# Hash attention with a gated feed-forward on one core: loads by need on the Pool queue, an eight-tile hash with four bit transfers, one piece of work held back at each block end, and first products placed behind the normalise

## Chip, core, metric

One core of one Trainium2 chip. The metric is the device time of a whole execution in microseconds (us), median of several. The profile's span, from first to last instruction, is 1.7 to 2.1 us shorter than the time of the same execution in the runs shown here.

## The reference, cut to what matters

```python
q_bits = (einsum('bhsd,dk->bhsk', q, proj) > 0); k_bits = ...      # 6 bits per row: a bucket
mask   = q_bucket[..., :, None] == k_bucket[..., None, :]
scores = where(mask, q @ k.T / sqrt(64), -1e9); attn = softmax(scores) @ v
x = attn, heads joined                                             # (3072, 512)
ffn = gelu(x @ w_gate) * (x @ w_val) @ w_out
out = x + sigmoid(x @ w_res) * ffn
```

Four batches, eight heads, 768 positions, head size 64, all fp32 outside the kernel.

## The kernel before

A *pair* is two heads of one batch: 16 pairs. `prep_pair` transposes a pair's q and k on TensorE, hashes them, and builds for each head an augmented matrix: 64 rows of q and k and 7 rows of bits, so that a single product yields score and mask together. The bits are computed across partitions 0 to 127 and must move to partitions 64 to 70: that needs transfers.

A *block* is one batch and half of the queries: 24 attention steps, `scores(i)` then `attend(i-2)`. At a block's end its output is transposed (`transpose_x`) and goes through 12 gate groups; the rest of its feed-forward is cut in pieces and dealt out over the next block's steps. Block 0 has no feed-forward to deal out. The *normalise* divides a pair's finished products by their row sums on VectorE (`rec`, then `xtok`).

The profile names tiles: `sc` are scores, `e` their exponentials on ScalarE, `av` products, `tps` transposes of q and k, `hps` the hash, `aug` the augmented matrix, `xps` the transposes of a block's output, which are copied to `xT`, `gps` gates, and `vps`, `rps`, `ops` the rest of the feed-forward.

```python
load_pair(0)                     # q, k, v on the SP queue
... proj on the ACT queue ...
load_pair(1)

def prep_pair(n):
    ...                          # 12 transposes, copies to trT on ScalarE and VectorE
    hp = mm_psum.tile(...)       # mm_psum has three buffers
    for i in range(4):           # q and k of two heads: four column tiles of 32
        matmul(hp[32*i:32*i+32, 0:CH], proj_pair, trT[:, i*CH:(i+1)*CH])
    tensor_scalar(bits, hp, 0.0, shift, is_gt, subtract)
    for hh, side, par in ...:    # eight transfers
        (scalar if n == 0 and par == 1 else sync).dma_start(a[D:KAUG, ...], bits[row:row+7])
    ...                          # VectorE casts of trT to the 64 upper rows: 4 of 64x768

cast_v(0); drain(prep_pair(0)); cast_v(1); drain(prep_pair(1))
load_pair(2); load_pair(3)       # behind the bit transfers on SP
...
if end_of_block:                 # in the step loop, after attend
    fill(0.8); transpose_x(u); fill(100.0)    # transpose_x: both copies on VectorE
    for m in range(KF): gate(u, m)
    ff = feed_forward(u)         # its last piece ends in y, o on VectorE and a store
```

The softmax here doesn't subtract the row's maximum and nothing guards it: scores larger than these inputs give would overflow.

Of the kernel before, what the change touches and what calls it, by code (L numbers as in the profile page):

```python
# [19 lines left out]
def kernel(  # L20
# [54 lines left out]
    def load_pair(n):  # L75
        b, j = pairs[n]
        for nm, src in (("q", q), ("k", k), ("v", v)):
            s = stage.tile([P, 2, T, D], FP32, tag=nm + "s", name=nm + "s")
            nc.sync.dma_start(
                s, src[b, 2 * j:2 * j + 2].rearrange("h (p t) d -> p h t d", t=T))  # L80
            staged[(nm, n)] = s

    load_pair(0)


# [6 lines left out]
    nc.scalar.dma_start(proj_pair[D:2 * D, NR:NR + NBITS], proj)  # L92
    load_pair(1)

    ind = const.tile([P, 2], FP32, name="ind")
    for side in range(2):
        nc.vector.tensor_reduce(
            ind[:, side:side + 1],
            ident.rearrange("p (h s c) -> p h s c", h=2, s=2)[:, :, side, NBITS:2 * NR:NR],
            axis=AX.XY, op=ALU.add)  # L100
# [7 lines left out]
    NAUG = 2 * H  # L108
    augs = [const.tile([P, 2 * S], BF16, name=f"aug{i}") for i in range(NAUG)]
# [6 lines left out]
    def aug_of(b, h):  # L116
        return augs[(b * H + h) % NAUG]

# [26 lines left out]
    def prep_pair(n):  # L145
# [15 lines left out]
        hp = mm_psum.tile([P, 512], FP32, tag="mm", name="hps")  # L161
        for i in range(4):
            nc.tensor.matmul(hp[32 * i:32 * i + 32, 0:CH], proj_pair, trT[:, i * CH:(i + 1) * CH],  # L163
                             start=True, stop=True)
        bits = s_pool.tile([P, CH], BF16, tag="bits", name="bits")
        nc.vector.tensor_scalar(bits, hp[:, 0:CH], 0.0, shift, op0=ALU.is_gt, op1=ALU.subtract)  # L166
        for hh in range(2):
            a = aug_of(b, 2 * j + hh)
            for side in range(2):
                for par in range(2):  # L170
                    row = 32 * (2 * hh + side) + NR * par
                    eng = nc.scalar if n == 0 and par == 1 else nc.sync
                    eng.dma_start(  # L173
                        a[D:KAUG, side * S + par * CH:side * S + (par + 1) * CH],
                        bits[row:row + NR, :])
        if n == 0:
            cast_aug(n, trT, 0)
            yield
            cast_aug(n, trT, 1)
            return  # L180
        yield
        cast_aug(n, trT, 0)
        yield
        cast_aug(n, trT, 1)
        yield

    def cast_aug(n, trT, hh):
        b, j = pairs[n]
        a = aug_of(b, 2 * j + hh)
        for par in range(2):  # L190
            nc.vector.tensor_scalar_mul(  # L191
                a[0:D, :].rearrange("d (s n) -> d s n", s=2)[:, :, par * CH:(par + 1) * CH],
                trT[par * D:(par + 1) * D, hh * S:(hh + 1) * S].rearrange("d (s n) -> d s n", s=2),
                QKS)
# [5 lines left out]
    LEAD = 2  # L200
    x_tok, xT, gh = {}, {}, {}
    e_tiles, av_tiles = {}, {}

    def scores(i):
        b, c, j, hh, jp = steps[i]
        a = aug_of(b, 2 * j + hh)
        sp = sc_psum.tile([P, 2, 512], FP32, tag="sc", name="sc")
        for x in range(2):
            jt = 2 * jp + x
            nc.tensor.matmul(sp[:, x, 0:CH], a[0:KAUG, S + jt * P:S + (jt + 1) * P],  # L210
                             a[0:KAUG, c * CH:(c + 1) * CH], start=True, stop=True)
        e = e_pool.tile([P, 2, CH], BF16, tag="e", name="e")
        nc.scalar.activation(e, sp[:, :, 0:CH], AF.Exp, scale=EXPS)  # L213
        e_tiles[i] = e
# [30 lines left out]
    def transpose_x(u):  # L245
        xT[u] = x_pool.tile([P, KM, CH], BF16, tag="xT", name="xT", bufs=2)
        for k2 in range(KM // 2):
            ps = mm_psum.tile([P, 1024], BF16, tag="mm", name="xps")
            for x in range(2):
                for t in range(TC):  # L250
# [3 lines left out]
            nc.vector.tensor_copy(xT[u][:, 2 * k2:2 * k2 + 2, :].rearrange("p k n -> p (k n)"),  # L254
                                  ps[:, 0:2 * CH])
# [52 lines left out]
    drain(prep_pair(0))  # L308
    cast_v(1)
    drain(prep_pair(1))  # L310
    load_pair(2)
    load_pair(3)
    run(weights)
    run(weights)


    begin = {2: 1, 3: 7}
    for n in range(4, len(pairs)):
        b, j = pairs[n]
        begin[n] = (b - 1) * 2 * LB + (LB + 6 * j if b == 1 else 12 * j)  # L320
    loads = {}
    for n in range(4, len(pairs)):
        loads.setdefault(max(2, begin.get(n - 3, -6) + 5), []).append(n)

    NS = len(steps)
    RATE = 17.0 / LB
    prep = None
# [3 lines left out]
    ff_next = None  # L331

    def fill(need):

        nonlocal ff
        while need > 0 and ff is not None:
            d = run(ff)
            if d is None:
                ff = None
            else:  # L340
                need -= d
        return need

    for i in range(NS + LEAD):
        if i < NS:
            scores(i)
        if i >= LEAD:
            attend(i - LEAD)

        for n in loads.pop(i, []):  # L350
            load_pair(n)
        if i < 14 * 2 and i % 2 == 0:
            run(weights)
        if prep is None and todo and i >= begin[todo[0]]:
            n = todo.pop(0)
            cast_v(n)
            prep = prep_pair(n)
        if prep is not None:
            if next(prep, "done") == "done":
                prep = None  # L360

        credit += RATE
        if credit > 0:
            credit = fill(credit) if ff is not None else 0.0
        if i >= LEAD and (i - LEAD) % LB == LB - 1:
            u = (i - LEAD) // LB
            fill(0.8)
            transpose_x(u)
            fill(100.0)
# [3 lines left out]
            credit = 0.0  # L373
    drain(ff)
# [30 lines left out]
```

## Time and profile before

| | before |
|---|---|
| time, median of 3 | 413.34 us (412.99 to 416.0) |
| span of the profiled run | 410.1 us |
| TensorE busy | 366.4 us, 89% |
| ScalarE / VectorE / GpSimd busy | 61% / 42% / 6% |
| first scores start | 16.03 us |
| first gate group starts | 64.18 us |

TensorE is the bound, so the thing to look for is where it is not at work, or at work slowly. The *chain of work* is followed back from the last instruction, at each step to what released it. PEclk is the TensorE clock that was granted, as a share of full speed. The ends of matmuls are modelled and overlap the next start.

### The profile page before, as it was taken

The numbers are of one execution on the slowest core, as the hardware profiler recorded it, in microseconds if no ns is written. First come the engines' busy times: TensorE is split into PE (matmuls) and PEld (weight loads), VectorE is DVE, ScalarE is ACT, GpSimd is POOL, SyncE is SP. The second block draws the span as 40 slices with busy tenths as digits, with TensorE's granted clock in tenths as the row PEclk, the third lists the DMA queues.
The fourth block names the chain that finished last, engine by engine and source line by source line (L and its number), as shares of the span: only waits on it lengthen the run. The fifth ranks groups of instructions, "written<-read, shape, count | busy, mean of one in ns | idle before, by whom it ended". The sixth has DMA issues, their size and how long they took to land.

```text
span 410.1 us, 7658 instructions
## 1 busy us (share of the span) xinstructions
PE 366.4 (89%) x3077; PEld 222.5 (54%) x3104; DVE 171.6 (42%) x328; ACT 248.6 (61%) x360; POOL 22.9 (6%) x35
## 2 busy tenths in 40 slices
PE   5348589999989998999989998999999999998995
PEld 3035255655556655565555655565556555654552
DVE  2504302675535654175326453275315331534162
ACT  2226557765657666766857666766767776775510
POOL 1225010001010000000000000000000000000000
PEclk9658859999999999999999999999999999999999
DMA  6669990034611114030500301000100010000001
GB/s 230 121 245 260 247 235 2 3 122 155 225 55 59 62 53 146 1 108 16 170 26 5 119 30 53 0 7 4 56 26 2 11 42 27 2 21 33 27 0 77
DMA packets 21779, 31.59 MB, mean 77 GB/s; under 512 B 2416, under 2 KB 17648, under 8 KB 21744
## 3 DMA queue, kind: packets, MB, share of 16 engines
q1 hardware_dynamic: 18248, 25.84, 18.4%
q0 software_dynamic: 3280, 5.24, 7.1%
q8 instruction: 24, 0.39, 0.4%
q14 instruction: 11, 0.09, 0.1%
q10 hardware_dynamic: 216, 0.02, 0.0%
HBM read 29.36 MB, written 6.29 MB: 87 GB/s over the span
## 4 chain that ended last, share of the span: by engine, by line
PE 80%; DVE 10%; DMA 4%; SPq 2%; issue 2%; ACTq 1%; ACT 0%; DVEq 0%
PE gps L262 16%; PE ops L287 14%; PE sc L210 14%; PE vps L272 13%; PE av L230 8%; PE tps L155 6%; PE rps L280 5%; PE hps L163 4%; DVE aug L191 2%; DMA aug<-bits 2%; DMA ks<-in_k_dram 2%; DVE gh L275 2%; SPq L173 2%; DVE y L292 1%; DVE o L294 1%
## 5 line engine op out<-in xcount | busy, mean ns | idle before, releaser
L213 ACT ACTIVATE e<-sc 128x768 bf16<-128x768 f32 x192 | 153.3, 811 | 73.4 <-PE sc L210 72.9
L210 PE MATMUL sc<-aug 71*128 71x384 bf16 x384 | 98.8, 340 | 6.6 <-DMA aug<-bits 5.5
L275 DVE TENSOR_TENSOR gh<-vps,gh 128x384 bf16<-128x384 f32 x96 | 53.0, 557 | 102.2 <-PE vps L272 89.3
L230 PEld LDWEIGHTS <-e 128*128 128x128 bf16 x1152 | 62.0, 100 | 34.7 <-issue 6.0
L272 PE MATMUL vps<-xT,wv 128*128 128x384 bf16 x384 | 75.2, 326 | 0.0
L262 PE MATMUL gps<-xT,wg 128*128 128x384 bf16 x384 | 64.8, 326 | 10.4 <-DVE xT L254 10.4
L230 PE MATMUL av<-vaug,e 128*128 128x65 bf16 x1152 | 68.5, 197 | 4.2 <-DVE xtok L240 3.9
L287 PE MATMUL ops<-wo,gh 128*128 128x512 bf16 x273 | 68.9, 379 | 0.6 <-issue 0.2
L264 ACT ACTIVATE gh<-gps 128x384 bf16<-128x384 f32 x96 | 47.1, 491 | 36.7 <-PE gps L262 36.7
L210 PEld LDWEIGHTS <-aug 71*128 71x128 bf16 x384 | 37.2, 102 | 37.1 <-DMA aug<-bits 5.6
L262 PEld LDWEIGHTS <-wg 128*128 128x128 bf16 x384 | 37.5, 98 | 36.3 <-issue 13.0
L272 PEld LDWEIGHTS <-wv 128*128 128x128 bf16 x384 | 33.2, 98 | 18.8 <-issue 3.8
L287 PEld LDWEIGHTS <-gh 128*128 128x128 bf16 x288 | 25.3, 98 | 24.1 <-issue 3.1
L191 DVE TENSOR_SCALAR aug<-trT 64x768 bf16<-64x768 f32 x64 | 37.0, 578 | 0.5
L292 DVE SCALAR_TENSOR_TENSOR y<-th,ops 128x512 f32<-128x512 bf16 x24 | 16.5, 688 | 45.8 <-PE ops L287 40.8
L155 PE MATMUL tps<-ident,qs 128*128 128x128 f32 x96 | 21.2, 311 | 12.6 <-DMA qs<-in_q_dram 12.6
L159 ACT COPY trT<-tps 128x512 f32<-128x512 f32 x32 | 18.6, 586 | 21.2 <-issue 9.2
L283 ACT ACTIVATE th<-rps 128x512 bf16<-128x512 f32 x24 | 14.3, 597 | 20.9 <-PE rps L280 20.5
L143 POOL CAST vaug<-vs 128x768 bf16<-128x768 f32 x16 | 14.2, 887 | 206.3 <-DMA vs<-in_v_dram 158.9
L280 PE MATMUL rps<-wr,xT 128*128 128x512 bf16 x84 | 23.4, 379 | 0.5
L166 DVE TENSOR_SCALAR bits<-hps,shift 128x384 bf16<-128x384 f32 x16 | 9.9, 617 | 30.1 <-PE hps L163 29.3
L155 PE MATMUL tps<-ident,ks 128*128 128x128 f32 x96 | 20.8, 306 | 0.5 <-DMA ks<-in_k_dram 0.4
(31 smaller groups left out, 158.6 us busy)
## 6 DMA issues: line engine op xcount, KB each, us to landing
qs<-in_q_dram SPq DMA_DIRECT2D x16, 384.0 KB
ks<-in_k_dram SPq DMA_DIRECT2D x16, 384.0 KB
vs<-in_v_dram SPq DMA_DIRECT2D x16, 384.0 KB
out_dram<-o SPq DMA_DIRECT2D x24, 256.0 KB
aug<-bits SPq DMA_DIRECT2D x124, 5.2 KB
wg<-in_moe_w_gate_dram POOLq DMA_DIRECT2D x4, 384.0 KB, 6.4
wv<-in_moe_w_val_dram POOLq DMA_DIRECT2D x4, 384.0 KB, 11.4
wo<-in_moe_w_out_dram POOLq DMA_DIRECT2D x4, 384.0 KB, 19.8
```

The costliest lines, as they stand in the source:

```text
L155: nc.tensor.transpose(ps[:, i * P:(i + 1) * P], tiles[4 * g + i], ident)
L191: nc.vector.tensor_scalar_mul(a[0:D, :].rearrange("d (s n) -> d s n", s=2)[:, :, par * CH:(par + 1) * CH], trT[par * D:(par + 1) * D, hh * ...
L210: nc.tensor.matmul(sp[:, x, 0:CH], a[0:KAUG, S + jt * P:S + (jt + 1) * P], a[0:KAUG, c * CH:(c + 1) * CH], start=True, stop=True)
L213: nc.scalar.activation(e, sp[:, :, 0:CH], AF.Exp, scale=EXPS)
L230: nc.tensor.matmul(av[:, o:o + D + 1], e[:, x, t * P:(t + 1) * P], va[:, 2 * j + hh, TS[jt], :], start=(first and x == 0 and t == 0), stop ...
L262: nc.tensor.matmul(ps[:, 0:CH], wg[:, kk, m * P:(m + 1) * P], xT[u][:, kk, :], start=(kk == 0), stop=(kk == KM - 1))
L264: nc.scalar.activation(gh[u][:, m, :], ps[:, 0:CH], AF.Gelu)
L272: nc.tensor.matmul(ps[:, 0:CH], wv[:, kk, m * P:(m + 1) * P], xT[u][:, kk, :], start=(kk == 0), stop=(kk == KM - 1))
L275: nc.vector.tensor_mul(sl, ps[:, 0:CH], sl)
L280: nc.tensor.matmul(rps, xT[u][:, kk, t * P:(t + 1) * P], wr[:, kk, :], start=(kk == 0), stop=(kk == KM - 1))
L287: nc.tensor.matmul(ops, gh[u][:, kk, t * P:(t + 1) * P], wo[:, kk, :], start=(kk == 0), stop=(kk == KF - 1))
L292: nc.vector.scalar_tensor_tensor(y, th, 1.0, ops, op0=ALU.add, op1=ALU.mult)
```

## The change

Intent: have pair 2 and later loaded before they are needed, and off the queue that the bits use; halve the bit transfers, by hashing the two 64-row halves on separate row tiles of the array, so that the two halves of a head's bits lie side by side in the same partitions; and leave TensorE something to do while the last transposes are copied.

```diff
-    load_pair(0)                              # q, k, v
-    ... load_pair(1) ...
+    load_pair(0, nc.sync, "qk"); load_pair(1, nc.sync, "qk")
+    load_pair(0, nc.sync, "v");  load_pair(1, nc.sync, "v")
...
+    load_pair(2, nc.gpsimd)                   # before any preparation
...
-        hp = mm_psum.tile([P, 512], FP32, tag="mm", name="hps")
+        hp = [mm_psum.tile([P, 512], FP32, tag="mm", name="hps") for _ in range(2)]
         for i in range(4):
-            matmul(hp[32*i:32*i+32, 0:CH], proj_pair, trT[:, i*CH:(i+1)*CH])
-        tensor_scalar(bits, hp[:, 0:CH], ...)
-        ... eight transfers of 7 rows x 384
+            for par in range(2):
+                matmul(hp[par][32*i:32*i+32, 0:CH], proj_pair[par*D:(par+1)*D, :],
+                       trT[par*D:(par+1)*D, i*CH:(i+1)*CH])
+        for par in range(2):
+            tensor_scalar(bits[:, par, :], hp[par][:, 0:CH], ...)
+        ... four transfers of 7 rows x 768
-        ... four casts of 64x768
+        ... two casts of 64x1536
...
-            nc.vector.tensor_copy(xT ..., ps)
+            copy = nc.vector.tensor_copy if k2 == 0 else nc.scalar.copy
...
-    load_pair(2); load_pair(3)                # after both preparations
+    load_pair(3, nc.gpsimd)                   # between them; later pairs on Pool too
-        begin[n] = (b-1)*2*LB + (LB + 6*j if b == 1 else 12*j)
+        begin[n] = (b-1)*2*LB + (LB + 6 + 6*j if b == 1 else 8 + 12*j)
-        attend(i - LEAD)
+        # the first product of each pair comes one step later, behind the normalise
-            fill(0.8); transpose_x(u); fill(100.0)
+            fill(99.0, NPIECES - 1); transpose_x(u); fill(99.0, NPIECES)
```

The weights keep to the Pool queue, in larger batches. The number of pieces dealt out over a block's steps is capped, so that three are left for its end.

More of the change, by code (lines that the diff above doesn't have):

```diff
@@ L73, with load_pair @@
     staged = {}
-    def load_pair(n):
+    def load_pair(n, eng, which="qkv"):
         b, j = pairs[n]
-        for nm, src in (("q", q), ("k", k), ("v", v)):
+        for nm in which:
+            src = {"q": q, "k": k, "v": v}[nm]
             s = stage.tile([P, 2, T, D], FP32, tag=nm + "s", name=nm + "s")
-            nc.sync.dma_start(
-                s, src[b, 2 * j:2 * j + 2].rearrange("h (p t) d -> p h t d", t=T))
+            eng.dma_start(s, src[b, 2 * j:2 * j + 2].rearrange("h (p t) d -> p h t d", t=T))
             staged[(nm, n)] = s
-    load_pair(0)
+    load_pair(0, nc.sync, "qk")
+    load_pair(1, nc.sync, "qk")
+    load_pair(0, nc.sync, "v")
+    load_pair(1, nc.sync, "v")
     ident = const.tile([P, P], FP32, name="ident")
@@ L91 @@
     nc.scalar.dma_start(proj_pair[0:D, 0:NBITS], proj)
-    nc.scalar.dma_start(proj_pair[D:2 * D, NR:NR + NBITS], proj)
-    load_pair(1)
+    nc.scalar.dma_start(proj_pair[D:2 * D, 0:NBITS], proj)
     ind = const.tile([P, 2], FP32, name="ind")
@@ L98 @@
             ind[:, side:side + 1],
-            ident.rearrange("p (h s c) -> p h s c", h=2, s=2)[:, :, side, NBITS:2 * NR:NR],
+            ident.rearrange("p (h s c) -> p h s c", h=2, s=2)[:, :, side, NBITS:NR],
             axis=AX.XY, op=ALU.add)
@@ L106 @@
     nc.vector.tensor_copy(ident_bf, ident)
-    NAUG = 2 * H
-    augs = [const.tile([P, 2 * S], BF16, name=f"aug{i}") for i in range(NAUG)]
+    load_pair(2, nc.gpsimd)
+    NAUG = 2 * NPAIR
+    augs = [const.tile([P, 2, 2 * S], BF16, name=f"aug{i}") for i in range(NAUG)]
     vaugs = []
@@ L114, with aug_of @@
         vaugs.append(va)
-    def aug_of(b, h):
-        return augs[(b * H + h) % NAUG]
+    def aug_of(b, j):
+        return augs[(b * NPAIR + j) % NAUG]
     wg = const.tile([P, KM, DFF], BF16, name="wg")
@@ L160, in prep_pair @@
             yield
-        hp = mm_psum.tile([P, 512], FP32, tag="mm", name="hps")
+        hp = [mm_psum.tile([P, 512], FP32, tag="mm", name="hps") for _ in range(2)]
         for i in range(4):
-            nc.tensor.matmul(hp[32 * i:32 * i + 32, 0:CH], proj_pair, trT[:, i * CH:(i + 1) * CH],
-                             start=True, stop=True)
-        bits = s_pool.tile([P, CH], BF16, tag="bits", name="bits")
-        nc.vector.tensor_scalar(bits, hp[:, 0:CH], 0.0, shift, op0=ALU.is_gt, op1=ALU.subtract)
@@ L167, in prep_pair @@
-        for hh in range(2):
-            a = aug_of(b, 2 * j + hh)
-            for side in range(2):
-                for par in range(2):
-                    row = 32 * (2 * hh + side) + NR * par
-                    eng = nc.scalar if n == 0 and par == 1 else nc.sync
-                    eng.dma_start(
-                        a[D:KAUG, side * S + par * CH:side * S + (par + 1) * CH],
-                        bits[row:row + NR, :])
-        if n == 0:
-            cast_aug(n, trT, 0)
-            yield
-            cast_aug(n, trT, 1)
-            return
@@ L181, in prep_pair @@
-        yield
-        cast_aug(n, trT, 0)
-        yield
-        cast_aug(n, trT, 1)
-        yield
-    def cast_aug(n, trT, hh):
-        b, j = pairs[n]
-        a = aug_of(b, 2 * j + hh)
+            for par in range(2):
+                nc.tensor.matmul(hp[par][32 * i:32 * i + 32, 0:CH], proj_pair[par * D:(par + 1) * D, :],
+                                 trT[par * D:(par + 1) * D, i * CH:(i + 1) * CH], start=True, stop=True)
+        bits = s_pool.tile([P, 2, CH], BF16, tag="bits", name="bits")
@@ L190, in cast_aug @@
+        for par in range(2):
+            nc.vector.tensor_scalar(bits[:, par, :], hp[par][:, 0:CH], 0.0, shift,
+                                    op0=ALU.is_gt, op1=ALU.subtract)
+        a = aug_of(b, j)
+        for i in range(4):
+            eng = nc.scalar if n == 0 and i % 2 == 1 else nc.sync
+            eng.dma_start(a[D:KAUG, i // 2, (i % 2) * S:(i % 2 + 1) * S], bits[32 * i:32 * i + NR])
         for par in range(2):
             nc.vector.tensor_scalar_mul(
-                a[0:D, :].rearrange("d (s n) -> d s n", s=2)[:, :, par * CH:(par + 1) * CH],
@@ L193, in cast_aug @@
-                trT[par * D:(par + 1) * D, hh * S:(hh + 1) * S].rearrange("d (s n) -> d s n", s=2),
-                QKS)
+                a[0:D].rearrange("d h (s p n) -> d (h s) p n", s=2, p=2)[:, :, par, :],
+                trT[par * D:(par + 1) * D, :].rearrange("d (i n) -> d i n", i=4), QKS)
+            if n > 0 and par == 0:
+                yield
+        yield
     steps = [(b, c, j, hh, jp) for b in range(B) for c in range(2) for j in range(NPAIR)
@@ L200 @@
     LEAD = 2
+    PS = 2 * (T // 2)
     x_tok, xT, gh = {}, {}, {}
@@ L205, in scores @@
         b, c, j, hh, jp = steps[i]
-        a = aug_of(b, 2 * j + hh)
+        a = aug_of(b, j)[0:KAUG, hh, :]
         sp = sc_psum.tile([P, 2, 512], FP32, tag="sc", name="sc")
@@ L209, in scores @@
             jt = 2 * jp + x
-            nc.tensor.matmul(sp[:, x, 0:CH], a[0:KAUG, S + jt * P:S + (jt + 1) * P],
-                             a[0:KAUG, c * CH:(c + 1) * CH], start=True, stop=True)
+            nc.tensor.matmul(sp[:, x, 0:CH], a[:, S + jt * P:S + (jt + 1) * P],
+                             a[:, c * CH:(c + 1) * CH], start=True, stop=True)
         e = e_pool.tile([P, 2, CH], BF16, tag="e", name="e")
@@ L253, in transpose_x @@
                                         x_tok[u][:, t, ko * P:(ko + 1) * P], ident_bf)
-            nc.vector.tensor_copy(xT[u][:, 2 * k2:2 * k2 + 2, :].rearrange("p k n -> p (k n)"),
-                                  ps[:, 0:2 * CH])
+            copy = nc.vector.tensor_copy if k2 == 0 else nc.scalar.copy
+            copy(xT[u][:, 2 * k2:2 * k2 + 2, :].rearrange("p k n -> p (k n)"), ps[:, 0:2 * CH])
     def gate(u, m):
@@ L308 @@
     drain(prep_pair(0))
+    load_pair(3, nc.gpsimd)
     cast_v(1)
-    drain(prep_pair(1))
-    load_pair(2)
-    load_pair(3)
-    run(weights)
-    run(weights)
-    begin = {2: 1, 3: 7}
+    prep = prep_pair(1)
+    for _ in range(4):
+        run(prep)
+    for _ in range(KM):
+        run(weights)
+    begin = {2: 0, 3: 6}
     for n in range(4, len(pairs)):
         b, j = pairs[n]
-        begin[n] = (b - 1) * 2 * LB + (LB + 6 * j if b == 1 else 12 * j)
+        begin[n] = (b - 1) * 2 * LB + (LB + 6 + 6 * j if b == 1 else 8 + 12 * j)
     loads = {}
     for n in range(4, len(pairs)):
-        loads.setdefault(max(2, begin.get(n - 3, -6) + 5), []).append(n)
+        loads.setdefault(max(14, begin[n] - 14), []).append(n)
     NS = len(steps)
-    RATE = 17.0 / LB
-    prep = None
+    RATE = 15.8 / LB
     todo = list(range(2, len(pairs)))
@@ L330, with fill @@
     credit = 0.0
-    ff_next = None
-    def fill(need):
-        nonlocal ff
-        while need > 0 and ff is not None:
-            d = run(ff)
-            if d is None:
-                ff = None
-            else:
-                need -= d
+    pieces = 0
+    NPIECES = KF + TC * (1 + KF // 4)
+    def fill(need, upto=NPIECES - 3):
+        nonlocal pieces
+        while need > 0 and ff is not None and pieces < upto:
+            need -= next(ff)
+            pieces += 1
         return need
+    done = 0
     for i in range(NS + LEAD):
@@ L346 @@
             scores(i)
-        if i >= LEAD:
-            attend(i - LEAD)
+        upto = i - LEAD if (i - LEAD) % PS != 0 or i >= NS else i - LEAD - 1
+        while done <= upto:
+            attend(done)
+            done += 1
         for n in loads.pop(i, []):
-            load_pair(n)
-        if i < 14 * 2 and i % 2 == 0:
-            run(weights)
+            load_pair(n, nc.gpsimd)
         if prep is None and todo and i >= begin[todo[0]]:
@@ L356 @@
             cast_v(n)
+            if n <= 3:
+                for _ in range(5):
+                    run(weights)
             prep = prep_pair(n)
-        if prep is not None:
+        if prep is not None and ((i - LEAD) % PS != PS - 2 or i < LB) and (i - LEAD) % LB != LB - 1:
             if next(prep, "done") == "done":
@@ L362 @@
         credit += RATE
+        if (i - LEAD) % PS == PS - 1 and credit < 0.1:
+            credit = 0.1
         if credit > 0:
-            credit = fill(credit) if ff is not None else 0.0
+            credit = min(fill(credit), 0.5)
         if i >= LEAD and (i - LEAD) % LB == LB - 1:
             u = (i - LEAD) // LB
-            fill(0.8)
+            fill(99.0, NPIECES - 1)
             transpose_x(u)
-            fill(100.0)
+            fill(99.0, NPIECES)
             for m in range(KF):
@@ L373 @@
             credit = 0.0
+            pieces = 0
     drain(ff)
```

## The prediction

> **What bounds the kernel now.** I read the page's slices first, for where the time is lost, then busy time by stage, then TensorE's waits, then the timeline around the start and around one block end.
>
> The kernel runs eight blocks (four batches, two halves of the queries). A block has 24 attention steps, then 12 gate groups; the rest of its feed-forward is spread over the next block's steps. The gate groups of blocks 0 to 7 start at 64.18, 115.18, 161.30, 207.24, 253.24, 298.24, 339.00 and 379.04 us in the timeline.
>
> The slices (10.25 us each) show TensorE's busy share and its granted clock:
>
> ```profile
> PE   5348589999989998999989998999999999998995
> PEclk9658859999999999999999999999999999999999
> ```
>
> After the sixth slice TensorE is full and at full clock. Before that it is half idle and half slow. The stage table splits this: the first three rows are blocks 1 to 3 (gate to gate), the last is block 0 from the first scores to the first gate; columns are length, then busy time of PE, PEld, DVE, ACT, POOL, then PEclk, DMA share and GB/s.
>
> ```profile
> 64.18:115.18 51.00, 48.20 (x417) 29.46 (x421) 27.22 (x50) 32.54 (x49) 4.05 (x4) 1.00 0.33 107
> 115.18:161.30 46.12, 44.54 (x392) 27.91 (x396) 22.65 (x44) 31.45 (x46) 1.00 (x2) 1.00 0.21 72
> 161.30:207.24 45.94, 44.22 (x385) 27.09 (x389) 20.86 (x41) 30.98 (x45) 2.50 (x3) 1.00 0.22 72
> 16.03:64.18 48.15, 29.89 (x258) 19.50 (x257) 13.91 (x28) 24.34 (x32) 10.44 (x15) 0.66 0.90 223
> ```
>
> Blocks 1 to 3 are bound by TensorE, with 1.6 to 2.8 us idle each. Block 0 holds no feed-forward, yet lasts as long: 18.3 us idle, and the busy part is at clock 0.66. TensorE's waits say what the idle time is for (total us, times, longest):
>
> ```profile
> PE tps L155 <- DMA qs<-in_q_dram: 12.6, 2, 8.6
> PE gps L262 <- DVE xT L254: 10.4, 8, 1.4
> PE sc L210 <- DMA aug<-bits: 5.5, 1, 5.5
> PE av L230 <- DVE xtok L240: 3.9, 5, 1.6
> PE hps L163 <- ACT trT L159: 3.5, 1, 3.5
> ```
>
> The 8.6 is pair 2's transposes, first in TensorE's order, waiting for pair 2's load. That load sits on the SP queue behind eight bit transfers; 5.5 is pair 3's bits, the same queue after it:
>
> ```profile
> 16.79 0.69 SPq L173
> ...
> 21.93 0.69 SPq L173
> 22.66 0.45 SPq L79
> 23.16 3.82 DMA ks<-in_k_dram
> ...
> 44.86 8.07 DMA aug<-bits
> 52.97 0.82 PE sc L210 x2
> ```
>
> These are from the chain of work: eight issues of about 0.73 us each from start to start, only then pair 2's q and k. The 10.4 is at the block ends; the timeline around the third shows it:
>
> ```profile
> 157.59 1.67 PE L287 MATMUL ops<-wo,gh 128*128 128x512 bf16 x7
> 159.10 0.83 PE L252 MATMUL xps<-ident_bf,xtok 128*128 128x128 bf16 x12
> 159.37 0.69 DVE L292 SCALAR_TENSOR_TENSOR y<-th,ops 128x512 f32<-128x512 bf16 x1 [0.88 <-PE ops L287]
> 160.09 0.69 DVE L294 SCALAR_TENSOR_TENSOR o<-y,xtok 128x512 f32<-128x512 f32 x1
> 160.70 1.01 DVE L254 COPY xT<-xps 128x768 bf16<-128x768 bf16 x2
> 161.30 2.41 PE L262 MATMUL gps<-xT,wg 128*128 128x384 bf16 x13 [1.37 <-DVE xT L254]
> ```
>
> VectorE does y and o of the last output tile before it copies the transposes, and TensorE has no work left meanwhile.
>
> **What the Trainium skill says.** "TensorE: Matmul & The Clock Gate", Part 3, says that matmuls on distinct row and column tiles of the array run together, measured at 10.6 times for 16 tiles. The trace agrees for the four column tiles of before: the hash is 8 recorded matmuls of 510 ns median (4.1 us if in a row), and takes 0.78 us on the chain of work (131.66 to 132.44). Row tiles, which the change adds, no line here shows. Part 1 of that page says that the clock is halved until TensorE has been busy for some 3.4 us and falls back after idleness. The trace agrees in kind: score pairs take 0.64 us of the chain at 54 to 60 us and 0.33 us in later blocks. "DMA: Bandwidth & Descriptors", section "Issuing engines are not separate DMA queues", says that moving a transfer to another issuing engine saves only sequencer time. Here that time is what hurts: 0.73 us an issue, with loads behind bits in order. The bandwidth is not gained.
>
> **The change, part by part.**
>
> (1) The start, to the first scores, 16.03 us before. Both pairs' q and k now lead the SP queue. Pair 0's hash ended at 8.76. The bits become two VectorE operations of about 0.62 us (the row of line 166 has 617 ns) instead of one: ready at 10.0 instead of 9.4. ScalarE issues two bit transfers, not four, each 0.78 us: free at 11.6 instead of 13.4. It then copies two pieces of pair 1 (1.07 us), pair 1's hash follows at 12.7 and takes 1.5 to 2.0 us at the slow clock, and the scores behind it start at about 14.6. Gain 1.4.
>
> (2) Block 0, 48.15 us before. The load of pair 2 goes out on the Pool queue before anything else there, so the 8.6 goes. Four bit transfers on SP instead of eight, and no loads between them: 4 x 0.73 = 2.9 us, plus 1.3 for the bits and 2.3 from the last issue to landing (before: last issue at about 50.6, scores released at 52.97) gives 6.5 to 7.2 us from hash to scores. The hash of pairs 2 and 3 is seven steps ahead of their scores, and a step takes 0.81 us (ScalarE's exponential) to 0.97 us (slow clock, spacing at 56 to 60 us), so 5.7 to 6.8 us. I allow 2 us of waits in all in place of the 5.5. The first product of a new pair is delayed by one step, behind the normalise: of the 3.9 us, 2.8 lie in block 0 and go. What remains is the work: 29.89 busy, less 1.7 us for eight of pair 4's transposes, which move into block 1, plus the 2 us of waits, plus 0.7 at the block end, where no feed-forward exists to fill: 30.9, say 30.5. The first gate is at 14.6 + 30.5 = 45.1 instead of 64.18.
>
> (3) Blocks 1 to 7 and the tail, 410.1 - 64.18 = 345.9 us. At each of seven block ends one piece of four output matmuls (0.86 us on the chain) is held back and issued after the transposes; the second xT copy goes to ScalarE, and y and o go behind the first on VectorE. From the start of the transposes, TensorE is busy for 0.8 + 0.86 = 1.65 us. The first copy (half of 1.01) begins after six transposes, ready at about 1.0. The ScalarE copy begins at 0.9 and takes about as long as the exponential over as many elements (0.81): ready at 1.75, needed by the third gate matmul at 2.0. So 7 x 1.37 = 9.6 goes; I give back 0.2 each for delays of semaphores and queues, 1.4. One wait on the normalise at 92.58 (1.07) goes. Pair 4's eight transposes add 8 x 0.11 = 0.9. Twelve hashes on eight tiles at about 0.1 us more each for double the instructions add 1.2. Together 345.9 - 9.6 + 1.4 - 1.1 + 0.9 + 1.2 = 338.7.
>
> The larger VectorE casts (64 rows, 1536 elements instead of two of 768, 578 ns each) and the extra bits operation cost VectorE roughly 0.3 us a pair; at 42% busy that is beside the path. The slower dispensing of feed-forward pieces moves work to the block end but keeps its sum.
>
> Sum: 45.1 + 338.7 = 383.8 us of span. Runs are longer than the span by 1.8 (profiled run: 411.9) to 3.2 (median). That gives 386; since every stall removed in block 0 should leave the clock high for longer, which I counted as nothing, I take 2 off: 384.
>
> **Rivals.**
>
> The clock rival: block 0 stays slow throughout, because attention alone is too thin to raise it. For it: at 53 to 60 us TensorE had hardly an idle moment and scores still took 0.64 us a pair. Then 24 x 0.97 plus 8.6 us for two slow preparations is 32 us, plus waits 34.5: 388. Against it: at 32 to 36 and 42 to 47 us, after transposes and hash, the pairs took 0.33. If it stays fast, ScalarE bounds at 24 x 0.81 + 4 x 0.59 = 21.8 us, 24 to 25 with waits: 378.
>
> The tile rival: row tiles do not run together. The hash doubles, 0.78 us for each of 14 pairs beyond the start: 11 us more, 394. Besides, the hash now holds two of the three PSUM buffers until two VectorE operations are done; a matmul group behind it might wait 0.6 us per pair, 7 us. Against it is the skill's figure; nothing in the trace decides it.
>
> The transfer rival: everything large now goes through Pool in order, with the casts of v between. The waits of POOL show output weights held for 0.8 and 2.3 us by older loads. If gate weights came late, the first gate would wait. By the queues' shares: 25.84 MB on q1 took 18.4% of 410 us with all 16 engines, so four pairs of 1.18 MB take 13.8 us; all weights took 7.1%, 29.1 us, and the gate's are 3 parts of 10 of them, 8.7 us; together with 2 us to start, some 25 us, against a gate at 45. So the transfer should be hidden; if not, 5 us more.
>
> **Range and chances.** The clock moves it by -6 to +4, the tiles by 0 to +11 (one chance in six), the block ends by -1.4 to +4, the transfers by 0 to +5. The range 375 to 394 holds most of these. To be within 2% of before, 405 us, three of them would have to go wrong at once: faster 0.96, same 0.03, slower 0.01.
>
> **What would show it.** Right, if the waits of TensorE have no line of over 2 us for qs, the first gate starts at 40 to 49 us, the gates' wait on xT is under 2 us in total, and a hash takes 0.8 to 1.0 us at full clock. Wrong, if the gates wait for y (a PSUM buffer) instead of xT, if a hash takes 1.5 us, if scores wait over 3 us for bits in block 0, or if block-to-block spacing from 115 us on stays at 46.

## The result, and the profile after

385.94 us, median of four runs (385.15 to 388.1), against 413.16 us of four runs of the kernel before: ratio 0.9336, 95% interval 0.9278 to 0.9393. A ratio here is the mean time of one kernel's fast runs over that of the other's of the same rounds, so it is not quite the ratio of the medians. The profiled run took 386.51 us, with a span of 384.7.

The same slices as before (now of 9.6 us), TensorE's busy share and clock:

```profile
PE   5768799999999999999999999999999999999995
PEclk9987579999999999999999999999999999999999
```

The full part starts one slice earlier, and the stretch before it is fuller, yet the clock still sinks to 0.5. The stages, cut as before: block 0 from the first scores to the first gate, block 1 and block 3 from gate to gate (columns: length, then busy time of PE, PEld, DVE, ACT, POOL, then PEclk, DMA share, GB/s):

```profile
16.27:51.84 35.57, 27.25 (x272) 17.53 (x266) 13.55 (x23) 22.32 (x30) 18.87 (x26) 0.74 1.10 247
51.84:98.01 46.17, 45.96 (x417) 28.46 (x416) 20.73 (x36) 33.45 (x49) 9.87 (x13) 0.98 0.33 110
...
145.24:189.11 43.87, 43.87 (x406) 27.12 (x404) 21.03 (x37) 31.45 (x47) 6.01 (x8) 1.00 0.22 75
```

| | before | after | forecast |
|---|---|---|---|
| first scores | 16.03 | 16.27 | 14.6 |
| block 0, from there to the first gate | 48.15 | 35.57 | 30.5 |
| from the first gate to the end of the span | 345.9 | 332.9 | 338.7 |
| span | 410.1 | 384.7 | 383.8 |

So 12.3 of the 25.4 us came out of the start and block 0, and 13.1 out of everything behind it. TensorE's waits (total us, times, longest), the whole list:

```profile
PE sc L200 <- DMA aug<-bits: 5.4, 2, 3.0
PE tps L158 <- DMA qs<-in_q_dram: 5.0, 2, 4.1
PE av L220 <- DVE xtok L230: 1.7, 2, 1.0
PE sc L200 <- ACT e L203: 1.2, 3, 0.6
PE tps L158 <- DMA ks<-in_k_dram: 0.2, 1, 0.2
```

The waits of the gates for xT (10.4 us before) are gone altogether. Pair 2's load is gone too: the 4.1 here is the very first load, at the start. The wait for bits has not shrunk (5.5 before, 5.4 now); it is two waits instead of one. The changed kernel run again has 3.8 us in two waits for bits, and a third wait of 3.6 us at pair 1's scores for which the list names no releaser; it also has one wait of 0.4 us of a gate for xT.

The block end, in the timeline of block 3, to set beside the one in the prediction:

```profile
185.85 1.89 PE L277 MATMUL ops<-wo,gh 128*128 128x512 bf16 x8
187.57 0.83 PE L242 MATMUL xps<-ident_bf,xtok 128*128 128x128 bf16 x12
188.11 0.56 DVE L245 COPY xT<-xps 128x768 bf16<-128x768 bf16 x1 [0.79 <-PE xps L242]
188.25 1.03 PE L277 MATMUL ops<-wo,gh 128*128 128x512 bf16 x4
188.44 0.80 ACT L245 COPY xT<-xps 128x768 bf16<-128x768 bf16 x1 [1.61 <-PE xps L242]
189.11 3.12 PE L252 MATMUL gps<-xT,wg 128*128 128x384 bf16 x18
189.38 0.69 DVE L282 SCALAR_TENSOR_TENSOR y<-th,ops 128x512 f32<-128x512 bf16 x1 [0.71 <-PE ops L277]
```

From the start of the transposes to the first gate matmul: 189.11 - 187.57 = 1.54 us, against 161.30 - 159.10 = 2.20 before, though 0.86 us of output matmuls now lie inside it. Like for like the gain is 0.66 + 0.86 = 1.52 us, not the 1.37 that the wait had recorded. The copies run side by side on VectorE and ScalarE while the held-back piece runs on TensorE; y and o come afterwards, and the gates do not wait for y.

### The profile page after: what moved, and what is told of

Same layout as the page of the kernel before. It is cut to its first block, busy times and chain, and to the rows that moved or that the text cites. A ratio compares the mean times of both kernels' runs of the same rounds, so it can differ in the third digit from the quotient of the medians.

```text
span 384.7 us, 7862 instructions
## 1 busy us (share of the span) xinstructions
PE 366.4 (95%) x3232; PEld 222.8 (58%) x3232; DVE 169.9 (44%) x304; ACT 252.7 (66%) x368; POOL 54.0 (14%) x77
## 4 chain that ended last, share of the span: by engine, by line
PE 91%; DMA 4%; DVE 2%; issue 1%; ACTq 1%; ACT 0%; SPq 0%; DVEq 0%
PE vps L262 16%; PE gps L252 16%; PE ops L277 16%; PE sc L200 16%; PE av L220 9%; PE tps L158 6%; PE rps L270 5%; PE hps L167 5%; DMA aug<-bits 3%; PE xps L242 2%; DVE bits L171 1%; DMA qs<-in_q_dram 1%; ACTq L176 1%; DVE aug L178 1%; DVE o L284 0%
## 5 line engine op out<-in xcount | busy, mean ns | idle before, releaser
L200 PE MATMUL sc<-aug 71*128 71x384 bf16 x384 | 97.1, 338 | 6.6 <-DMA aug<-bits 5.4
L220 PEld LDWEIGHTS <-e 128*128 128x128 bf16 x1152 | 58.2, 100 | 26.6 <-issue 3.1
L277 PE MATMUL ops<-wo,gh 128*128 128x512 bf16 x288 | 71.9, 379 | 0.0
L220 PE MATMUL av<-vaug,e 128*128 128x65 bf16 x1152 | 63.6, 197 | 1.8 <-DVE xtok L230 1.7
L254 ACT ACTIVATE gh<-gps 128x384 bf16<-128x384 f32 x96 | 45.5, 491 | 11.5 <-PE gps L252 10.3
L171 DVE TENSOR_SCALAR bits<-hps,shift 128x384 bf16<-128x384 f32 x32 | 18.3, 612 | 41.0 <-PE hps L167 41.0
L178 DVE TENSOR_SCALAR aug<-trT 64x1536 bf16<-64x1536 f32 x32 | 30.8, 962 | 0.5
L80 POOL DMA_DIRECT2D qs<-in_q_dram x14 | 10.3, 736 | 137.3 <-PE tps L158 133.0
L270 PE MATMUL rps<-wr,xT 128*128 128x512 bf16 x96 | 24.7, 379 | 0.0
L160 DVE COPY trT<-tps 128x512 f32<-128x512 f32 x16 | 11.1, 691 | 23.7 <-PE tps L158 23.5
```

What stands on the lines that cost most here:

```text
L171: nc.vector.tensor_scalar(bits[:, par, :], hp[par][:, 0:CH], 0.0, shift, op0=ALU.is_gt, op1=ALU.subtract)
L178: nc.vector.tensor_scalar_mul(a[0:D].rearrange("d h (s p n) -> d (h s) p n", s=2, p=2)[:, :, par, :], trT[par * D:(par + 1) * D, :].rearra ...
L200: nc.tensor.matmul(sp[:, x, 0:CH], a[:, S + jt * P:S + (jt + 1) * P], a[:, c * CH:(c + 1) * CH], start=True, stop=True)
L220: nc.tensor.matmul(av[:, o:o + D + 1], e[:, x, t * P:(t + 1) * P], va[:, 2 * j + hh, TS[jt], :], start=(first and x == 0 and t == 0), stop ...
L254: nc.scalar.activation(gh[u][:, m, :], ps[:, 0:CH], AF.Gelu)
L270: nc.tensor.matmul(rps, xT[u][:, kk, t * P:(t + 1) * P], wr[:, kk, :], start=(kk == 0), stop=(kk == KM - 1))
```

## Experiments

All kernels gave correct results. The kernel before had a median of 413.1 us; "against the changed kernel" below is the difference of the ratio from 0.9348, that of the changed kernel run again, times 413.1. Single ratios have 95% intervals of about 1.0 to 2.4 us on either side. The first four runs, the rerun of the changed kernel among them, were on one chip, the next four on a second and the last four on a third; on the second and third the changed kernel itself was not run, so differences of under 2 us are not sure there.

### The changed kernel again

> The changed kernel itself, unedited, as the yardstick for the other three on this chip. Expected 385 to 388 us, ratio to the kernel before 0.93 to 0.94; first gate at about 52 us and block spacings of 43.9 us in blocks 3 to 5.

Measured 386.77 us, ratio 0.9348 (0.9323 to 0.9372); first gate at 52.30, spacings in blocks 3 to 5 of 43.9 us. It is the yardstick.

### Block ends undone

```diff
-            copy = nc.vector.tensor_copy if k2 == 0 else nc.scalar.copy
+            copy = nc.vector.tensor_copy
-            fill(99.0, NPIECES - 1); transpose_x(u); fill(99.0, NPIECES)
+            fill(99.0, NPIECES);     transpose_x(u)
```

> The changed kernel with the block ends as before: all feed-forward pieces before the transposes, both xT copies on VectorE behind y and o. Theory (the 13 us gained after the first gate come mainly from the block ends; the stall from the last transpose to the first gate matmul was 1.55 us by start times, not the recorded 1.37): 7 x 1.55 = 11 us slower than the changed kernel, 396 to 398 us, with the gates waiting for xT again about 1.4 us each. Rival (the gain comes from the preparations moved away from the block starts and from the delayed first product of each pair): at most 4 us slower.

Measured 399.07 us, ratio 0.9651: 12.5 us slower, 1.8 us for each of the seven ends. Its list of TensorE's waits has the old one back:

```profile
PE gps L252 <- DVE xT L245: 9.6, 7, 1.4
```

The rival falls. In the profile 344.5 us lie behind the first gate (398.9 - 54.38), against 332.6 in the rerun of the changed kernel: 11.9 us, nearly all of the 13.1. The order at the block ends is the largest single part of the gain. Reading the recorded wait (7 x 1.37 = 9.6) understates it by 2 to 3 us. The edit undoes two things at once, the held-back piece and the copy on ScalarE; which of them is worth how much is not separated.

### Hash of before

```diff
-        # in words: two row tiles x four column tiles, four transfers
+        # in words: four column tiles, eight transfers (as before); casts as changed
```

> The changed kernel with the hash of before: four column tiles, one bits operation, eight bit transfers a pair; all else as changed. Theory (the transfers' issue time sits in front of block 0's scores, the tiles themselves are neutral for TensorE): hash at full clock again 0.78 us against 0.80, so nothing after the first gate (within 1 us), and block 0 longer by up to 4 x 0.73 = 2.9 us for each of pairs 1 to 3, less 0.5 each for the bits operation saved: 4 to 8 us slower in total. Rival (the landing of the bits is delayed by the other transfers on the same DMA engines, not by the number of issues): within 2 us of the changed kernel.

Measured 389.42 us, ratio 0.9411: 2.6 us slower, between the rival's 2 and the theory's 4. Nothing of it lies behind the first gate (331.8 us from there to the end, against 332.6 in the rerun), so eight tiles are neutral for TensorE. The first gate comes at 53.92 us instead of 52.30, but the profile does not show that the transfers did this: pair 0's k came 2.25 us late there and 0.54 in the rerun, block 0 is no longer (36.2 us against 36.5), and its wait for bits, 6.7 us in all, lies between the 5.4 of the first profile and the 7.4 of the rerun if that one's nameless wait is counted. With some 1.9 us of noise on either side of the difference the run does not decide between theory and rival, and where the 2.6 us are lost is not shown. The tiles themselves, at full clock, by the timelines of the kernel before and, in the second fence, of the changed one:

```profile
131.59 0.85 PE L163 MATMUL hps<-trT,proj_pair 128*32 128x384 f32 x8
132.37 0.82 PE L272 MATMUL vps<-xT,wv 128*128 128x384 bf16 x4
```

```profile
166.17 0.88 PE L167 MATMUL hps<-trT,proj_pair 64*32 64x384 f32 x16
166.97 0.82 PE L262 MATMUL vps<-xT,wv 128*128 128x384 bf16 x4
```

Start to start: 0.78 us for eight records, 0.80 for sixteen. (Each of these fp32 matmuls leaves two records: a pair's hash is four matmuls before and eight after.)

### Loads on the SP queue, in the new order

```diff
-    load_pair(2, nc.gpsimd); load_pair(3, nc.gpsimd); ... load_pair(n, nc.gpsimd)
+    load_pair(2, nc.sync);   load_pair(3, nc.sync);   ... load_pair(n, nc.sync)
```

> The changed kernel with pairs 2 to 15 loaded from the SP queue, at the same places in program order; weights stay on Pool. Theory A (the order of need removed the 8.6 us wait, the queue is indifferent): within 3 us of the changed kernel, either way; pair 2's load then stands behind pair 1's on one queue, so that the small projection load may land before 8.5 us and the first scores come 1 us earlier. Theory B (the Pool queue is what matters, because loads that wait for a staging buffer hold up the bit transfers behind them on SP): more than 4 us slower, with TensorE waiting for bits in later blocks.

Measured 392.1 us, ratio 0.9493: 6.0 us slower, but the profiled run was the fastest of five, 387.99 us, and shows TensorE waiting 4.5 us for bits in two waits, none in a later block. By time theory B holds; its reason is not shown. The list has no wait for pair 2's q either, so in this profile the order of need alone took the 8.6 us away. What can be said is that the queue is not indifferent, and that the four slower runs, 391.75 to 393.15 us, left no trace.

### Pairs 2 and 3 loaded late, as before

```diff
-    load_pair(2, nc.gpsimd)          # first on Pool
-    load_pair(3, nc.gpsimd)
     for _ in range(KM): run(weights)
+    load_pair(2, nc.sync); load_pair(3, nc.sync)
```

> The changed kernel with the loads of pairs 2 and 3 back where they stood before: on the SP queue, behind pair 1's bit transfers. Theory (the order of need is what took the wait of 8.6 us away): pair 2's transposes wait again, less long than before as four transfers and not eight stand ahead; its q issued at about 20.5, landed at 24 to 25, where the transposes started at 19: 4 to 7 us slower than the changed kernel. Rival (block 0 has slack elsewhere, for example the bits of pair 1 are then released sooner because no bulk load competes with them): within 2 us.

Measured 391.8 us, ratio 0.9488: 5.8 us slower, in the theory's range. The wait is back, 6.3 us for pair 2 in place of 8.6 of before:

```profile
PE tps L157 <- DMA qs<-in_q_dram: 10.3, 2, 6.3
```

The first gate moves to 58.34 us. The edit changes the queue of these two pairs along with their place, but the run before this one had the new place on the SP queue without that wait. So the order of need is a real part of the gain, here about as large as the wait.

### Weights behind pair 1's bits

```diff
     prep = prep_pair(1); ...
+    # in words: Pool copies 4 columns of each of pair 1's four landed bit transfers
     for _ in range(KM): run(weights)
```

> The changed kernel with one addition: Pool reads four corners of pair 1's landed bits before it issues the first weight load, so that no weight is in flight while those bits are. Theory (the bits of pair 1 land 4.1 us after their last issue because bulk transfers are ahead of them on the same engines): TensorE's wait of 2.5 to 3.0 us for them falls to 1.5 us or less, first gate 1 to 2 us earlier, total 1 to 2 us faster, unless a gate weight is then late. Rival (the latency is the transfers' own): wait unchanged, total the same or slower.

Measured 386.42 us, ratio 0.9356: no change in time (0.3 us). The mechanism, though, is as the theory had it. The chain of work of the changed kernel has the issue of pair 1's first transfer, then the second from its issue to its landing:

```profile
17.61 0.69 SPq L176
18.30 0.04 issue
18.35 6.19 DMA aug<-bits
24.54 0.09 issue
24.63 0.48 PE sc L200 x2
```

With the weights held back, SP issues the same four from 20.08 us on, 0.73 us apart, and Pool sees them one by one:

```profile
22.09 0.18 POOL L307 COPY bits_seen<-aug 7x4 bf16<-7x4 bf16 x1 [4.30 <-DMA aug<-bits]
22.77 0.18 POOL L307 COPY bits_seen<-aug 7x4 bf16<-7x4 bf16 x1 [0.50 <-DMA aug<-bits]
```

That is 2.0 us from issue to landing for the second (22.77 - 20.81) instead of 6.2, and TensorE's wait for pair 1's bits is gone (one wait for bits remains, 2.5 us, pair 3's). The late start of this run, told next, is a rival for both. It may explain the wait: with block ends undone the start was nearly as late (first scores at 18.27), and TensorE did not wait for pair 1's bits either. It does not explain the landing: there the four transfers, issued from 19.57 us on with the weights in flight, landed 5.4 to 6.2 us after their issue by the trace's semaphore events, while three additions together (below), with the weights held back and first scores at 15.80, has the first issued at 17.04 and seen by Pool at 19.04. The start of the profiled run was late: pair 0's k held TensorE up for 3.6 us, and the first scores came at 18.81. Since the addition reaches Pool only after that, the late start is not its doing; it is how far the start varies from run to run. In 8 of the 13 profiles with the new order of loads, TensorE waits over 0.9 us for pair 0's k; in the one of the kernel before, 0.16 us.

### The projection ahead of pair 2's load

```diff
+    nc.gpsimd.tensor_copy(proj_seen, proj_pair)
     load_pair(2, nc.gpsimd)
```

> The changed kernel with one addition: Pool reads the landed projection before it issues pair 2's load. Theory (the projection, tiny rows, landed at 8.5 us instead of before 7.2 because pair 2's load joined the two first pairs' on the same engines): pair 0's hash no longer waits for it, first scores 1 to 1.5 us earlier than 16.3, total 1 us faster; pair 2 must still land before 19 us. Rival (the projection's own latency): hash and total unchanged.

Measured 385.57 us, ratio 0.9344: 0.2 us faster, which is nothing. The profile has the hash of pair 0 done at 10.1 us as before: the wait for the projection is gone, but pair 0's k came 1.6 us late. First scores at 15.81, first gate at 49.98, some 2 us earlier than in the changed kernel; the times do not show it.

### Matmuls of no use against the slow clock

```diff
+    ones = const.tile([P, 512], BF16); memset(ones, 1.0)
+    warm(6)                                   # six 128x512 matmuls at the start
     ...
+        if i < LB: warm(1)                    # one in each step of block 0
```

> The changed kernel with matmuls of no use: six of 128x512 while the first load is on its way, and one in each of block 0's 24 steps. Theory (block 0 is partly bound by the slow clock, which more TensorE work raises): scores at 0.33 us a pair in all of block 0, granted clock above 0.9 there instead of 0.74, the hash of pair 0 at most 1 us once the projection is there, first gate 3 to 6 us earlier. Rival (ScalarE's exponentials and the waits for bits set block 0's length, so the clock is worth little): first gate within 1.5 us of before. If the clock does not rise, the extra matmuls cost up to 24 x 0.43 = 10 us.

Measured 386.4 us, ratio 0.9358: unchanged (0.4 us). The clock did rise; the slices and the stage from first scores to first gate:

```profile
PEclk9589999999999999999999999999999999999999
```

```profile
16.19:50.19 34.00, 27.48 (x296) 16.25 (x289) 13.56 (x23) 22.26 (x31) 18.18 (x25) 0.92 1.10 237
```

Clock 0.92 instead of 0.74, and block 0 is 34.0 us instead of 35.6: the first gate comes 1.65 us earlier, close to the rival's 1.5 and far from the theory's 3 to 6. That is a net figure, as the 24 added matmuls take TensorE's time too (9.79 us of recorded busy time); what the clock alone is worth is not separated. The gain lies at the end of block 0. From pair 3's scores to the transposes the changed kernel takes 7.90 us (42.41 to 50.31) at clock 0.50 without a recorded wait, this one 5.77 (42.91 to 48.68) at full clock. Over whole runs the clock says little: block 0 took 34.2 us at 0.71 (the projection ahead), 35.6 at 0.74 and 36.5 at 0.81 (the rerun).

### The first product of a pair in its own step

```diff
-        upto = i - LEAD if (i - LEAD) % PS != 0 or i >= NS else i - LEAD - 1
+        upto = i - LEAD
```

> The changed kernel with the first product of each pair in its own step again, not one step later. If the delay took the normalise waits away, as the prediction said (2.8 us in block 0, 1.1 later): 2 to 4 us slower than the changed kernel (386.8 on the first chip). If VectorE's order decides (bits and a 0.96 us cast stand ahead of the normalise, and 1.7 us of waits remain in the changed kernel anyway): within 1.5 us.

Measured 392.94 us, ratio 0.9511 over the fast runs: 6.7 us slower, more than either theory had. Where it was lost is open: the profile fell on an execution of 946.1 us, the one slow run of six, which cannot be compared. The trace of the kernel before gives a hint only. In block 3, where no wait is recorded, a pair's first product starts 0.63 us after its scores (178.66 to 179.29) instead of the usual 0.33. But behind the first gate only six of the 28 first products are late at all by their starts, 2.5 us in sum, 1.23 of them at one place (92.58). So of the 6.7 us most lies in block 0, or comes from the new surroundings; this is not shown.

### Preparations at the steps of before

```diff
-        begin[n] = ... (LB + 6 + 6 * j if b == 1 else 8 + 12 * j)
+        begin[n] = ... (LB + 6 * j     if b == 1 else 12 * j)
```

> The changed kernel with the preparations of pairs 4 to 15 begun at the steps of before (at the block's start and 6 steps earlier for batch 1). If the shift was worth what the blocks gained beyond their ends (about 0.3 to 0.5 us a block in blocks 1 to 5, a hash of 1.23 us at the block start instead of 0.8): 1 to 2.5 us slower. If not: within 1 us.

Measured 384.41 us, ratio 0.9295 (0.9252 to 0.9338): 2.2 us faster. From the first gate to the end its span has 383.8 - 52.80 = 331.0 us, against 332.9 and 332.6 in two profiles of the changed kernel. Its blocks 3 to 5 take 43.53 us each, against 43.86, 43.94 and 43.86 in both profiles of the changed kernel. So the shift of the preparations, and of the loads that go with it, did not pay, and by these profiles costs 1.6 to 1.9 us. As the interval of its time overlaps the changed kernel's, and the chips differ, it is the best version run here, not a proven one.

### Three additions together, and a fourth

```diff
+    projection first, weights behind pair 1's bits, matmuls of no use      # three_joined
+        if n > 0: yield          # before the casts in prep_pair           # four_joined
```

> The projection ahead of pair 2's load, the weights behind pair 1's bits, and the matmuls of no use in block 0, together. If the start, the bits and the clock are separate causes, their gains add: first gate at 46 to 48 us instead of 52, total 381 to 384 us. If block 0's length is set by the chain hash, bits, transfer, scores whatever the rest does: first gate at 50, total 385 to 387.

Measured 386.67 us, ratio 0.9342: no gain (0.2 us). The profiled run has its first gate at 48.77 us and a span of 381.3, so there the gains did add up; but of six runs two took 382.4 and 383.1 us, and four 386.6 to 387.2, and those left no trace. What separates the two kinds stays open; the record has a mean granted clock of 0.996 and 0.988 for the two, and 0.980 for each of the four.

> The same with one more: after a pair's bit transfers are issued, its two VectorE casts wait for the next step, so that in block 0 the normalise of the pair before comes ahead of bits and casts. Theory (the normalise waits of about 1 us each that remain are VectorE's order): those waits fall under 0.4 us each, total 1 to 2 us under three_joined. Rival (the hash then comes one step later and the bits with it): waits for bits grow by as much, no gain.

Measured 390.74 us, ratio 0.9456: 4.7 us slower than the three. The normalise waits vanished from the list, and the waits for bits took their place, as the rival said (3.5 us in all with three additions):

```profile
PE sc L213 <- DMA aug<-bits: 8.9, 3, 4.6
```

## Why the prediction was right, and where its steps were not

The time lay 2 us from the forecast, but that is not because every step was right: the first gate came 6.7 us later than forecast, and the rest took 5.8 us less. That the two errors nearly cancel is luck.

**The bound and the three places of loss: right.** Block 0 and the block ends are where the gain came from, in halves (12.3 and 13.1 us), and undoing one part at a time cost 12.5 us (block ends), 6.7 (first products), 5.8 (order of loads) and 2.6 (hash). That comes to 27.6 us, near the whole gain of 26.9, but two parts are missing from it: the shift of preparations, which costs, and the queue of the later loads, whose 6.0 us may overlap with the order.

**Part 1, the start: wrong by 1.7 us.** Two steps failed. The first is "Pair 0's hash ended at 8.76", taken over from before. Pair 2's load now shares the engines with the start, and TensorE's loads of the hash's weights waited for the projection (1.20 us, until 8.48), so the hash ended at 10.10. Holding pair 2's load back took that wait away, though pair 0's k was late in that run. The second is "two bit transfers, not four, each 0.78 us": ScalarE's first issue takes twice that, in the kernel before as in the changed one, on their chains of work:

```profile
9.43 1.58 ACTq L173
11.01 0.04 issue
11.05 0.74 ACTq L173
```

```profile
11.26 1.58 ACTq L176
12.84 0.04 issue
12.88 0.74 ACTq L176
13.62 0.04 issue
13.67 0.59 ACT trT L162
```

So ScalarE was free at 13.6 and not at 11.6: 1.2 us of that from the late bits, 0.8 from this. Pair 1's hash, forecast for 12.7, began at 14.30.

**Part 2, block 0: right about pair 2's load, wrong about the bits, 5.1 us short.** Pair 2's wait of 8.6 us went as forecast, and the busy part is 27.25 us for a predicted 28.2. The failed term is the waits. They fill the whole idle time of 8.3 us: 5.4 for bits, 1.7 for the normalise and 1.2 for exponentials, where the prediction allowed 2.0, nothing and nothing, and 0.7 for the block end, where none is recorded. (That is 5.6 more, less 0.9 of busy time, and 0.4 lost in rounding 30.9 to 30.5.) I allowed "2 us of waits in all" for bits, from 0.73 us an issue and "2.3 from the last issue to landing". That figure was a misreading: it runs from the issue of pair 3's seventh transfer (done at 50.58) to the landing of the third, for which the scores waited. The chain shown in the prediction has that one's own time, `44.86 8.07 DMA aug<-bits`: 8.07 us. In the changed kernel the transfers took 6.2 us (pair 1) and 4.8 (pair 3), and pair 1's 2.0 with the weights held back. So what costs is the landing among bulk loads more than the number of issues. I listed the transfer rival only for the gates, which never waited, and not for the bits. The second wrong term is the normalise: "2.8 lie in block 0 and go", but 1.7 stay. The larger cast, which I had called beside the path, stands on VectorE between the bits and the normalise; in the chain of work of the changed kernel:

```profile
26.73 0.61 DVE bits L171
27.34 0.86 DVE aug L178
28.20 0.11 DVE rec L229
28.31 0.02 issue
28.34 0.57 DVE xtok L230
```

Moving the casts away took the normalise waits with it, and the bits then came later: two waits trade places. That the chain hash, bits, transfer, scores is as long as block 0's steps allow would explain it; no run tests this apart.

**Part 3, behind the first gate: right in mechanism, 5.8 us short in size.** Three terms were too cautious. The 1.4 us that I gave back for delays were not needed: the trace has no gate wait left. The hash costs 0.02 us more and not 0.1, which is 1.0 us over twelve pairs. And the bubbles were 1.5 us by starts (1.7 to 1.8 by the experiment) rather than the recorded 1.37, 1 to 3 us over seven. What the delayed first products gave, I counted as one wait of 1.07; by their starts they were 2.5 us late in the kernel before, behind the first gate. Undoing them cost 6.7 us, though how much of that lies in block 0 is not shown. Against all this stands a cost that the prediction did not have, the shift of the preparations.

**The clock rival: half right.** The clock did stay low (0.74), and it did not matter much: raised to 0.92 by added matmuls it gave 1.6 us of block 0, net of these, and nothing measurable of the time. **The tile rival: wrong.** Sixteen records of 507 ns median fit in 0.80 us, and no wait for a PSUM buffer behind the hash is in the list. (Its sum, 384 and 11, makes 395 and not 394.) **The signs I named:** a first gate of 40 to 49 us did not come (51.84), and scores waited more than 3 us for bits, which I had named as a sign of being wrong; the gates' waits, the hash's length and the block spacing were as forecast. The list does have a line of over 2 us for qs, but that is the first load of all, which is there in the kernel before too.

## What to carry to other kernels

On an engine that is the bound, order the end of a stage so that one piece of its own work is held back to cover the copies, and give those copies to two engines ahead of anything that nobody waits for. Count such bubbles from start to start, as the recorded wait leaves part of them out. And a small transfer on the critical path wants the bulk loads out of its way: its landing time is not a constant but depends on what else is in flight (2.0 us against 6.2 here, though that gained no measured time).

## What the Trainium skill lacked or had wrong

- "DMA: Bandwidth & Descriptors", section "Anatomy of one DMA — SWDGE (gpsimd) path", gives some 2.0 us of fixed cost for a transfer issued from Pool. Small transfers issued from SP took as long here with the weights held back (2.0 us), but the page gives no figure for a small transfer among bulk loads: 6.2 and 4.8 us here, and 8.07 in the kernel before.
- "TensorE: Matmul & The Clock Gate", Part 3, has no fp32 case. Here eight fp32 matmuls on tiles of 64 rows by 32 columns, 384 columns streamed, take 0.80 us together, and four on tiles of 128 by 32 take 0.78.
- The same page, Part 1, says that sustained activity of some 3.4 us ends the slow clock, not how activity is weighed. In the changed kernel attention steps alone ran from 42.41 to 50.31 us without a recorded wait of TensorE, at a granted clock of 0.50 (0.64 us a score pair on the chain of work); with one 128x512 matmul more in each step it was 1.00 there. It mentions a clock stuck low for 50 us and more; one execution here was slow throughout, 946.1 us, a block's 48 gate matmuls taking 21.7 us instead of 7.8, while the records give a granted clock of 1.000.
